# Attention, expert layers and a gated MLP on one core: one early load for the hash, smaller first pieces, gate and identity in one product

## The chip, the cores and the metric

One core of one Trainium2 chip runs the whole program in one launch. The time is the device time in microseconds, taken as the median over runs. The engines are TensorE (PE in the rows, its weight loads PEld), VectorE (DVE), ScalarE (ACT), GpSimd (POOL) and the queue engine SyncE (SP), which only issues transfers.

## What is computed

Three layers follow each other, all in float32:

```python
q_bits = (einsum('bhsd,dk->bhsk', q, proj) > 0)      # 6 hash bits, k alike
mask = q_bucket[:, :, :, None] == k_bucket[:, :, None, :]
scores = where(mask, scale * q @ k.T, -1e9)           # B=2, H=8, S=768, D=64
x = softmax(scores) @ v                               # 1536 tokens of 512
noisy = x @ w_gate + log1p(exp(x @ w_noise)) * noise  # 8 experts, best two
x = sum over the two: weight * relu(x @ w1[e]) @ w2[e]
h = x @ w_in;  out = (h * sigmoid(1.702 * h)) @ w_out
```

## The kernel before

**Attention** works on eight pairs of heads (`n` = 0 to 7, heads `j` = 0, 1 in a pair). Scores are products of float32r parts: `u1`, `v1` (scaled q and k) hold the high parts on 128 partitions, `u2`, `v2` the corrections on 64 partitions and, on 12 more, the hash bits, scaled so that a differing bit puts a score out of reach. One step `g` (96 in all) takes one block of 128 queries of one head against all 768 keys: `a_score` issues two products with `u1`, `v1` and two with `u2`, `v2` (L310), `a_soft` reduces the maximum on DVE (L322) and makes a scale and a bias (L323, L324), `a_exp` runs the exponential on ACT (L333), `a_trans` turns the result with six transposes on PE (L350) and copies them out on ACT or DVE (a string `COPIES` says which), `a_av` multiplies with v (L360), 12 products for a query block of both heads, each two instructions in the trace. Scores run two steps ahead of the transposes.

The order on every engine is written out by hand: `attention` holds a table of (step, function, arguments), and within a step the table's calls follow the fixed calls above. An engine runs its instructions in that order.

**The first pair** has functions of its own (`z_...`), since its loads have just started. `a_load(0)` issues k of head 0 and then the hash matrix `projq` on ACT's queue, and on SP's queue the first half of q of head 0, k of head 1 and the other three halves of q. A column of ones (`sgn`) comes by POOL's queue. `z_mm` is the hash product of one half of one q or k (L191, 64 rows by 32 columns of PE, 384 columns moved), `z_bits` makes the bits of it on DVE (L263), for q with a scaling on ACT behind (L266). `z_u1`, `z_lo`, `z_u2`, `z_v1`, `z_v2` make the parts. Ahead of all this PE multiplies a matrix of ones with itself 27 times (`WARM`, L533).

**The later pairs** use `a_hash`, `a_hb` (bits on DVE, half of them scaled on ACT, L207) and DMAs that move the bits into `u2`, `v2`.

**The output steps** `a_xt` run 18 times: 15 take three row blocks, three (at the end) one. For each block a product of the attended values `xu` (weights of PE) with 32 columns of gate weights (L398, two instructions each) and one transpose of `xu` by the identity (L401, one instruction) go to one bank; DVE scales both by the softmax sums.

**Routing** of a group of 384 tokens runs in DVE operations between steps; POOL scatters token rows to expert slots by indirect DMAs (`r_scatter`).

**Expert 0** starts inside attention's scope: `f_load` fetches its 384 rows with one DMA, `f_tr` transposes them by column block (12 transposes, L999) into two tiles, ACT makes the high part (L793), DVE the rest (L794), and `f_s1` multiplies (through `m_mm1`, L1020 to L1022). Experts 1 to 7 and the last MLP follow; they hold PE from 265 us to the end.

Of the kernel before, what the change touches and what calls it, by code (L numbers as in the profile page):

```python
# [34 lines left out]
WARM = 27  # L35
W0 = 28
# [5 lines left out]
class Kernel:  # L42
# [19 lines left out]
    def consts(self):  # L62
        nc, a = self.nc, self.a
        p = self.cpool
        self.sc = self.t(p, [128, 2], F32, "sc")
# [3 lines left out]
        self.sgn = self.t(p, [128, 1], F32, "sgn")  # L69
        nc.gpsimd.dma_start(self.sgn, a["sgn"])  # L70
        self.ident = self.t(p, [128, 128], F32, "ident")
        make_identity(nc, self.ident)

    def consts2(self):
        nc, a = self.nc, self.a
        p = self.cpool
        self.wg = self.t(p, [128, 4, 32], F32, "wg")
        nc.gpsimd.memset(self.wg, 0.0)
        for j in range(2):
            for x, nm in enumerate(("w_gate", "w_noise")):  # L80
                c0 = 16 * j + 8 * x
                nc.sync.dma_start(self.wg[64 * j:64 * j + 64, :, c0:c0 + 8],
                                  a[nm].rearrange("(c j p) e -> j p c e", j=2, p=64)[j])
        self.tri = self.t(p, [128, 128], BF, "tri")
        nc.vector.memset(self.tri, 1.0)
        nc.gpsimd.affine_select(self.tri, self.tri, pattern=[[1, 128]], compare_op=ALU.is_gt,
                                fill=0.0, base=0, channel_multiplier=-1)
        self.ones = self.t(p, [128, 128], BF, "ones")
        nc.vector.memset(self.ones, 1.0)
# [4 lines left out]
        nc.vector.tensor_copy(self.iotb, self.iota)  # L94
        nc.vector.memset(self.iotb[:, 0:1], float(E * NT))
        self.over = self.t(p, [128, 9], F32, "over")
        nc.vector.memset(self.over, 0.0)
        nc.vector.memset(self.over[:, 0:1], float(CAP - CAPB))
        nc.vector.memset(self.over[:, 8:9], float(CAP - CAPA))
        self.slot = self.t(p, [128, 12, 2], I32, "slot")  # L100
        self.ysl = self.t(p, [128, 12, 2], I32, "ysl")
        self.slot2 = self.t(p, [128, 12, 2], I32, "slot2")
        self.wgt = self.t(p, [128, 12, 2], F32, "wgt")
        self.nz = self.t(p, [128, 12, 8], F32, "nz")
        nc.sync.dma_start(self.nz, a["noise"].rearrange("(i p) e -> p i e", p=128))
        self.spacer = self.t(p, [1, 1], F32, "spacer")
        self.macc = self.t(p, [128, 9], BF, "macc")
        nc.vector.memset(self.macc, 0.0)
# [20 lines left out]
    def a_load(self, n):  # L129
# [58 lines left out]
    def hash_mm(self, ps, r, hf, t):  # L188

        rs = slice(64 * hf, 64 * hf + 64)  # L190
        return self.nc.tensor.matmul(ps[r:r + 32, :], self.projq[rs, :], t[rs, hf * HALF:(hf + 1) * HALF],  # L191
                                     start=True, stop=True)
# [10 lines left out]
    def a_hb(self, n, hf):  # L203
        nc = self.nc
        hb = self.hb[n][:, hf * HALF:(hf + 1) * HALF]
        nc.vector.tensor_scalar(hb, self.hps[hf], 0.0, self.sgn[:, 0:1], op0=ALU.is_gt, op1=ALU.add)
        nc.scalar.activation(hb[64:128, :], hb[64:128, :].bitcast(F32), AF.Copy, scale=BIG)  # L207
        self.use(dve=0.62, act=0.4)
# [19 lines left out]
    def z_u1(self, j, hf, e):  # L228
        cs = slice(hf * HALF, (hf + 1) * HALF)
        self.z_mul(e, self.uv[0, j][0][:, cs], self.raw[0]["q", j][:, cs], self.sc[:, 0:1])  # L230

    def z_lo(self, j, hf, e):
        cs = slice(hf * HALF, (hf + 1) * HALF)
# [3 lines left out]
    def z_u2(self, j, hf, e):  # L237
        cs = slice(hf * HALF, (hf + 1) * HALF)
        self.z_mul(e, self.uv[0, j][2][0:64, cs], self.raw[0]["q", j][0:64, cs], SCALE)

    def z_v1(self, j, e):
        self.z_mul(e, self.uv[0, j][1], self.raw[0]["k", j], self.sc[:, 1:2])

    def z_v2(self, j, e):
        u1, v1, u2, v2 = self.uv[0, j]
        self.z_sub(e, v2[0:64, :], self.raw[0]["k", j][0:64, :], v1[0:64, :].bitcast(F32))
# [12 lines left out]
    def z_bits(self, nm, j, hf):  # L259
        nc = self.nc  # L260
        r = 64 * (nm == "k") + 32 * j
        d = self.uv[0, j][2 if nm == "q" else 3][64:76, hf * HALF:(hf + 1) * HALF]
        o = nc.vector.tensor_scalar(d, self.zps[hf][r:r + 12, :], 0.0, self.sgn[r:r + 12, 0:1], op0=ALU.is_gt, op1=ALU.add)  # L263
        self.z_other(o, r, hf, False)
        if nm == "q":
            nc.scalar.activation(d, d.bitcast(F32), AF.Copy, scale=BIG)  # L266
# [5 lines left out]
    COPIES = "aaddaaadaaaddaaaaaaaaadaadadadadaaddaddadaaadaaaaaadadaaaaaaaaaadddaaddaaadaaddaaaadaaadaadddaadaaaadaaaddaadadaaddadadaaaaaaaaaadaadaddaaaaaaaddaadaaaaaaaddaaaaaaaddaaaddaaaaaaaaaaaadaaaaaaaaaaaadaaddaaaaadaaa"  # L272
# [28 lines left out]
    def a_score(self, g):  # L301
# [6 lines left out]
        for (l, r, kk, st) in ((u1, v1, 128, True), (u2, v2, K2, False)):  # L308
            for hf in range(2):
# [64 lines left out]
    def a_xt(self, u, c=None, spare=False):  # L374
# [20 lines left out]
        pt = ps[:, 0:nch * 128].rearrange("p (c d) -> p c d", c=nch)  # L395
        pl = ps[:, 384:384 + nch * 32].rearrange("p (c j e) -> p c j e", c=nch, j=2)
# [1174 lines left out]
```

## Time and profile before

| What | us |
|---|---|
| median of three runs (865.27 to 866.52) | 865.75 |
| the profiled execution, device time | 869.32 |
| its span, first to last instruction | 867.5 |
| PE busy | 848.0 |
| DVE busy | 524.3 |
| ACT busy | 443.6 |
| POOL busy | 220.0 |

The mean granted clock of PE is 0.988 of full speed. The profile cuts the span into stretches and tells for each how long an engine was busy, which clock PE was granted and what the DMA engines moved; the chain that ended last follows the last instruction back, at each step to the one that released it. Attention ends at about 262 us.

### The profile page before, as it was taken

To read this page: it belongs to the slowest core of one execution; us is meant where nothing else is said; L and a number is where in the kernel's file an instruction comes from. 1 tells how busy PE (TensorE), PEld (TensorE's weight loads), DVE (VectorE), ACT (ScalarE), POOL (GpSimd) and SP (SyncE) were. 2 spreads that over 40 slices of the span, in tenths; PEclk is the share of its full clock that TensorE was granted. 3 is DMA by queue.
4 is the path that set the end of the run, shared out by engine and by line. 5 is a ranking of instruction groups with operands and counts; after the bars stand their busy time and mean duration, and the time that the engine had idled before them with its cause. 6 is when DMAs were issued, how large, how long until landed. Compare 5 with 4: busy or idle time off the path is not lost.

```text
span 867.5 us, 15554 instructions
## 1 busy us (share of the span) xinstructions
PE 848.0 (98%) x6116; PEld 777.5 (90%) x6116; DVE 524.3 (60%) x1068; ACT 443.6 (51%) x787; POOL 220.0 (25%) x227
## 2 busy tenths in 40 slices
PE   8999999999989999999999999999999999999997
PEld 5888898788979999999999999978898988989896
DVE  5877778676765598989898897756512121212120
ACT  4977988788763444443544344447423231314130
POOL 4421654486024000000000000026524141503040
PEclk6999999999999999999999999999999999999999
DMA  5747654533135577887878687638301010100000
GB/s 187 223 162 247 168 157 138 181 105 111 37 111 209 195 261 240 290 253 234 296 237 279 223 268 233 213 119 321 98 25 49 25 49 25 42 33 1 25 1 28
DMA packets 52382, 132.29 MB, mean 152 GB/s; under 512 B 8912, under 2 KB 11024, under 8 KB 52304
## 3 DMA queue, kind: packets, MB, share of 16 engines
q1 hardware_dynamic: 43968, 109.64, 38.6%
q0 software_dynamic: 6992, 20.37, 7.7%
q10 hardware_dynamic: 1344, 1.23, 0.4%
q8 instruction: 50, 0.82, 0.4%
q14 instruction: 28, 0.23, 0.1%
HBM read 92.05 MB, written 35.39 MB: 147 GB/s over the span
## 4 chain that ended last, share of the span: by engine, by line
PE 95%; ACT 1%; DMA 1%; DVE 1%; issue 1%; POOL 0%; ACTq 0%; DVEq 0%; POOLq 0%
PE g L1292 15%; PE s L310 9%; PE av L360 8%; PE p L350 7%; PE y L1044 5%; PE y L1046 5%; PE y L1045 5%; PE h L1020 5%; PE h L1021 5%; PE h L1022 5%; PE o L1337 4%; PE o L1339 4%; PE o L1338 4%; PE t L1063 2%; PE t L999 1%; PE m L398 1%
## 5 line engine op out<-in xcount | busy, mean ns | idle before, releaser
L322 DVE TENSOR_REDUCE mx<-s 128x1 f32<-128x768 f32 x96 | 91.5, 954 | 30.0 <-PE s L310 28.2
L333 ACT ACTIVATE P<-s,sm 128x768 f32<-128x768 f32 x96 | 95.3, 992 | 26.4 <-DVE sm L324 23.6
L1301 POOL TENSOR_TENSOR gl<-sg,gh 128x512 fp32r<-128x512 f32 x48 | 66.2, 1380 | 162.1 <-ACT gh L1300 162.1
L1245 POOL DMA_INDIRECT yg<-ys,ysl x24 | 25.8, 1074 | 304.1 <-DVE wl L893 297.7
L310 PE MATMUL s<-v,u 76*128 76x384 f32 (+1 forms) x384 | 95.6, 371 | 1.3 <-DVE v L263 0.8
L1297 DVE TENSOR_TENSOR sg<-g,sg 128x512 f32<-128x512 f32 x48 | 33.2, 692 | 93.5 <-ACT sg L1296 89.2
L350 PE MATMUL p<-ident,P 128*128 128x128 f32 x576 | 81.7, 278 | 4.4 <-ACT hh L281 2.4
L310 PEld LDWEIGHTS s<-v,u 76*128 76x128 f32 (+1 forms) x384 | 64.6, 195 | 17.9 <-issue 11.9
L350 PEld LDWEIGHTS p<-ident,P 128*128 128x128 f32 x576 | 69.7, 143 | 10.9 <-ACT hh L281 3.3
L1027 ACT ACTIVATE hh<-h 128x416 fp32r<-128x416 f32 x56 | 29.0, 518 | 72.7 <-PE h L1022 72.3
L1044 PE MATMUL y<-hh,wh 128*128 128x416 f32 (+1 forms) x144 | 51.2, 355 | 0.0
L1296 ACT ACTIVATE sg<-g 128x512 f32<-128x512 f32 x48 | 28.7, 599 | 41.9 <-PE g L1292 39.6
L1046 PE MATMUL y<-hh,wl 128*128 128x416 f32 (+1 forms) x144 | 49.8, 346 | 0.0
L1045 PE MATMUL y<-hl,wh 128*128 128x416 f32 (+1 forms) x144 | 49.7, 345 | 0.0
L1300 ACT ACTIVATE gh<-sg 128x512 fp32r<-128x512 f32 x48 | 30.3, 631 | 31.0 <-DVE sg L1297 30.2
L1028 DVE SCALAR_TENSOR_TENSOR hl<-h,hh 128x416 fp32r<-128x416 f32 x56 | 32.9, 588 | 14.2 <-ACT hh L1027 14.1
L1292 PE MATMUL g<-bth,wh 128*128 128x256 f32 x144 | 40.2, 279 | 0.0
L1292 PE MATMUL g<-btl,wh 128*128 128x256 f32 x144 | 40.1, 279 | 0.0
L1292 PE MATMUL g<-bth,wl 128*128 128x256 f32 x144 | 40.1, 278 | 0.0
L1292 PE MATMUL g<-x2h,wh 128*128 128x256 f32 x144 | 39.7, 277 | 0.0
L1044 PE MATMUL y<-hh,wxh 128*128 128x416 f32 (+1 forms) x112 | 39.6, 354 | 0.0
L1292 PE MATMUL g<-x2h,wl 128*128 128x256 f32 x144 | 39.6, 276 | 0.0
(327 smaller groups left out, 2492.4 us busy)
## 6 DMA issues: line engine op xcount, KB each, us to landing
ws<-in_w SPq DMA_DIRECT2D x40, 512.0 KB, 5.4
d_in<-in_w SPq DMA_DIRECT2D x32, 512.0 KB, 5.0
bth<-in_w SPq DMA_DIRECT2D x16, 512.0 KB, 4.1
btl<-in_w SPq DMA_DIRECT2D x16, 512.0 KB, 4.7
wd<-d_o SPq DMA_DIRECT2D x32, 256.0 KB, 4.0
xs<-xeh SPq DMA_DIRECT2D x13, 512.0 KB, 5.7
rawk<-in_kT SPq DMA_DIRECT2D x15, 384.0 KB, 4.2
rawq<-in_qT SPq DMA_DIRECT2D x14, 384.0 KB, 4.9
```

Source lines behind the costliest of these rows:

```text
L310: nc.tensor.matmul(ps[:, hf, :HALF], l[:kk, q0:q0 + 128], r[:kk, hf * HALF:(hf + 1) * HALF], start=st, stop=not st)
L322: nc.vector.tensor_reduce(mx, ps[:, :, :HALF], axis=AX.XY, op=ALU.max, negate=True)
L333: nc.scalar.activation(P, ps[:, :, :HALF], AF.Exp, bias=sm[:, 1:2], scale=sm[:, 0:1], accum_out=self.RS[u][:, c, j, 0:1])
L350: nc.tensor.transpose(ps[:, kb, :], P[:, hf, kb * 128:(kb + 1) * 128], self.ident)
L360: nc.tensor.matmul(self.pa[64 * j:64 * j + 64, c * 128:(c + 1) * 128], self.vt[n][:, kb, 64 * j:64 * j + 64], PT[:, j, kb, :], start=(kb = ...
L1020: nc.tensor.matmul(ps, wh[:, fs], xh[:, d, :n], start=(d == 0), stop=False)
L1021: nc.tensor.matmul(ps, wh[:, fs], xl[:, d, :n], start=False, stop=False)
L1044: nc.tensor.matmul(ps, wh[:, ds_], hh[:, f, :], start=(f == 0), stop=False)
L1045: nc.tensor.matmul(ps, wh[:, ds_], hl[:, f, :], start=False, stop=False)
L1046: nc.tensor.matmul(ps, wl[:, ds_], hh[:, f, :], start=False, stop=(f == 7))
L1292: nc.tensor.matmul(ps[:, x, :], self.units[NU + 4 * (f // 8) + d][w][:, fs], y[:, d, :], start=(i == 0), stop=(i == 11))
L1301: nc.gpsimd.tensor_tensor(gl[:, fo, :], g, gh[:, fo, :].bitcast(F32), op=ALU.subtract)
```

## The change

**Loads.** One array `hdr` (66 columns: the hash matrix twice, a threshold and a factor for the bits) is the first DMA of ACT's queue, then k of both heads. SP's queue brings the four halves of q, then one array `cst` with gate weights, identity and noise, then the second pair's loads, then v. The five small loads of gate weights and noise and the identity built on POOL are gone. DVE negates six columns of `hdr`.

**Bits.** Threshold and factor are read from `hdr`, so one DVE operation makes scaled bits; the scalings on ACT (L266, L207) are gone.

**Order of the start.** `WARM` is 37 and the ones are DVE's first instruction. The first half of q is worked on in pieces of 128 and 256 columns (`PIECE`), k in two halves. `keep_on` puts 26 more products of the ones behind the hash product of q's second half. Further calls of the table move by a step or two, one subtraction of pair 1 goes from DVE to POOL, and `COPIES` has other letters.

**Output steps.** One product of 160 columns (32 of gate weights and the identity side by side) takes the place of L398 and L401.

**Expert 0.** Three DMAs fetch its rows, `f_tr` transposes and splits by row tile, and the first product group takes its eight products with the high part first. The store of the last group's rows moves behind `f_s1(0)`.

```diff
-WARM = 27
+WARM = 37
...
+        self.ones = self.t(p, [128, 128], BF, "ones")
+        nc.vector.memset(self.ones, 1.0)
...
-        nc.gpsimd.dma_start(self.sgn, a["sgn"])
-        make_identity(nc, self.ident)
+        nc.vector.tensor_scalar(self.hdr[:, NB:32 + NB], self.hdr[:, NB:32 + NB], -1.0, None, op0=ALU.mult)
...
+        cst = self.t(p, [128, 384 + 96], F32, "cst")
+        nc.sync.dma_start(cst, a["cst"])
+        self.iw = [cst[:, 192 * (c // 2) + 32 * (c % 2):192 * (c // 2) + 32 * (c % 2) + 160] for c in range(4)]
+        self.ident = cst[:, 32:160]
...
-            nc.scalar.dma_start(raw["k", 0], a["kT"][b, 2 * p])
-            nc.scalar.dma_start(self.projq, a["projq"])
-            for nm, j, c0, c1 in (("q", 0, 0, HALF), ("k", 1, 0, S), ("q", 1, 0, HALF), ("q", 0, HALF, S), ("q", 1, HALF, S)):
+            nc.scalar.dma_start(self.hdr, a["hdr"])
+            for j in range(2):
+                nc.scalar.dma_start(raw["k", j], a["kT"][b, 2 * p + j])
+            for nm, j, c0, c1 in (("q", 0, 0, HALF), ("q", 1, 0, HALF), ("q", 0, HALF, S), ("q", 1, HALF, S)):
...
+    PIECE = (slice(0, 128), slice(128, HALF), slice(HALF, S))
...
+    def keep_on(self, n):
+        ps = self.t(self.ps_p, [128, 128], F32, "p")
+        for _ in range(n):
+            self.nc.tensor.matmul(ps, self.ones, self.ones, start=True, stop=True)
...
+        o = nc.vector.tensor_scalar(d, ps, self.hdr[r:r + 12, 64:65], self.hdr[r:r + 12, 65:66], op0=ALU.is_gt, op1=ALU.mult)
...
-            nc.scalar.activation(d, d.bitcast(F32), AF.Copy, scale=BIG)
...
         for x in range(nch):
-            nc.tensor.matmul(ps[:, 384 + 32 * x:416 + 32 * x], xu[:, x * 128:(x + 1) * 128], self.wg[:, p, :],
-                             start=True, stop=True)
-        for x in range(nch):
-            nc.tensor.transpose(pt[:, x, :], xu[:, x * 128:(x + 1) * 128], self.ident)
+            nc.tensor.matmul(pc[:, x, :], xu[:, x * 128:(x + 1) * 128], self.iw[p], start=True, stop=True)
...
+        for i in range(3):
+            self.nc.sync.dma_start(t[:, i, :], x[i * 128:(i + 1) * 128, :])
...
+        for i, (o, w) in enumerate(self.tiles(0)):
...
+            for d in range(4):
+                nc.tensor.transpose(pt[:, d, :], self.xrow[0][:, i, d * 128:(d + 1) * 128], self.ident)
+            nc.scalar.activation(xh[:, :, o:o + w], pt[:, :, :w], AF.Copy)
...
+        if e == f == 0:
+            mm.sort(key=lambda m: m[2] is xl)
```

The table's effect on the order, at the three places that count. **PE, from the first hash product to the third block of scores.** `m` and `av` are the two banks of hash results, `s` a block of scores, `p` a spare bank. Before:

```order
L191 MATMUL m_194<-rawq_1_105,projq_80 32x384
L191 MATMUL av_96<-rawk_1_106,projq_80 32x384
L191 MATMUL m_194<-rawk_1_106,projq_80 32x384
L191 MATMUL m_194<-rawk_1_108,projq_80 32x384
L191 MATMUL av_96<-rawk_1_108,projq_80 32x384
L310 MATMUL s_212<-v_1_190,u_1_185 128x384 x2
L310 MATMUL s_212<-v_1_191,u_1_186 128x384 x2
L191 MATMUL m_194<-rawq_1_107,projq_80 32x384
L310 MATMUL s_230<-v_1_190,u_1_185 128x384 x2
L310 MATMUL s_230<-v_1_191,u_1_186 128x384 x2
L191 MATMUL av_96<-rawq_1_105,projq_80 32x384
L310 MATMUL s_249<-v_1_192,u_1_187 128x384 x2
```

Now:

```order
L185 MATMUL m_189<-rawk_1_106,hdr_80 32x384
L185 MATMUL m_189<-rawq_1_105,hdr_80 32x384
L185 MATMUL av_96<-rawk_1_106,hdr_80 32x384
L185 MATMUL m_189<-rawk_1_108,hdr_80 32x384
L185 MATMUL av_96<-rawk_1_108,hdr_80 32x384
L185 MATMUL m_189<-rawq_1_107,hdr_80 32x384
L320 MATMUL s_216<-v_1_185,u_1_180 128x384 x2
L320 MATMUL s_216<-v_1_186,u_1_181 128x384 x2
L320 MATMUL s_233<-v_1_185,u_1_180 128x384 x2
L320 MATMUL s_233<-v_1_186,u_1_181 128x384 x2
L185 MATMUL av_96<-rawq_1_105,hdr_80 32x384
L253 LDWEIGHTS ones_116
```

A sixth hash product (q of head 1, first half) now stands ahead of the first scores, two blocks of scores stand together, and 26 products of the ones stand between them and the third.

**SP, its first transfers.** `rawq`, `rawk` with 1_105 to 1_108 are the first pair's, with 2_ the second's. Before:

```order
L138 DMA rawq_1_105<-in_qT 128x384
L138 DMA rawk_1_108<-in_kT 128x768
L138 DMA rawq_1_107<-in_qT 128x384
L138 DMA rawq_1_105<-in_qT 128x384
L138 DMA rawq_1_107<-in_qT 128x384
L82 DMA wg_127<-in_w_gate 64x4x8
```

Now:

```order
L131 DMA rawq_1_105<-in_qT 128x384
L131 DMA rawq_1_107<-in_qT 128x384
L131 DMA rawq_1_105<-in_qT 128x384
L131 DMA rawq_1_107<-in_qT 128x384
L77 DMA cst_124<-in_cst 128x480
L137 DMA rawq_2_302<-in_qT 128x768
```

k of head 1 has gone to ACT's queue (third there), and the second pair's loads stand where the small gate loads stood.

**PE, from the last output steps to expert 0.** Before:

```order
L398 MATMUL m_3782<-wg_127,xu_3746 128x32
L401 MATMUL m_3782<-ident_122,xu_3746 128x128
L398 MATMUL p_3792<-wg_127,xu_3780 128x32
L401 MATMUL p_3792<-ident_122,xu_3780 128x128
L999 MATMUL s_3804<-ident_122,xrow_1_3653 128x128 x6
L999 MATMUL s_3813<-ident_122,xrow_1_3653 128x128 x6
L1020 MATMUL s_3836<-xeh_3802,wh_1403 128x320
L1021 MATMUL s_3836<-xel_3803,wh_1403 128x320
```

Now:

```order
L410 MATMUL m_3753<-cst_124,xu_3718 128x160
L410 MATMUL p_3761<-cst_124,xu_3751 128x160
L818 MATMUL s_3771<-cst_124,xrow_1_3624 128x128 x4
L818 MATMUL s_3778<-cst_124,xrow_1_3624 128x128 x4
L818 MATMUL p_3785<-cst_124,xrow_1_3624 128x128 x4
L1048 MATMUL s_3806<-xeh_3769,wh_1412 128x320
L1048 MATMUL s_3806<-xeh_3769,wl_1413 128x320
```

One product has taken the place of two, the transposes come in three groups of four, and the products with the low part `xel` have moved behind eight with the high part.

## Rows read from the trace of the kernel before

**Rows 1.** The page, part 1: engine, busy us (share of the span), instructions.
```profile
PE 848.0 (98%) x6116; PEld 777.5 (90%) x6116; DVE 524.3 (60%) x1068; ACT 443.6 (51%) x787; POOL 220.0 (25%) x227
```

**Rows 2.** Timeline of PE at the start: start, length, line, shapes, [idle before <-releaser].
```profile
1.65 2.99 PE L533 MATMUL s<-ones 128*128 128x128 bf16 x27 [1.65 <-DVE ones L89]
6.34 0.48 PE L191 MATMUL m<-rawq,projq 64*32 64x384 f32 x1 [1.70 <-DMA projq<-in_projq]
...
7.13 0.62 PE L310 MATMUL s<-v,u 128*128 128x384 f32 x2
8.58 1.13 PE L310 MATMUL s<-v,u 76*128 76x384 f32 x2 [0.83 <-DVE v L263]
```

**Rows 3.** Windows of the start: length, busy PE, PEld, DVE, ACT, POOL, PEclk, DMA, GB/s.
```profile
2.00:4.00 2.00, 2.00 (x22) 2.00 (x20) 0.34 (x6) 1.05 (x1) 1.18 (x6) 1.00 0.96 260
4.00:6.00 2.00, 0.64 (x7) 0.44 (x5) 0.88 (x2) 1.18 (x2) 0.00 (x0) 1.00 0.89 328
6.00:8.00 2.00, 1.41 (x12) 0.49 (x12) 0.81 (x3) 0.44 (x2) 1.66 (x1) 0.96 0.83 215
7.80:8.00 0.20, 0.00 (x0) 0.00 (x0) 0.18 (x1) 0.18 (x1) 0.20 (x1) 0.61 0.61 34
...
21.40:21.60 0.20, 0.20 (x2) 0.20 (x1) 0.20 (x1) 0.20 (x1) 0.00 (x0) 0.76 0.00 0
```

**Rows 4.** Chain that ended last, 9 to 26 us: start, length, work.
```profile
9.71 1.42 PE m L191 x2
11.13 1.58 PE s L310 x4
...
15.70 1.28 PE p L350 x6
...
22.81 0.70 PE s L310 x4
23.51 0.66 PE p L350 x6
24.17 1.46 PE av L360 x24
```

**Rows 5.** DVE's groups by form, 0 to 60 us: busy us, mean ns, idle before.
```profile
L322 DVE TENSOR_REDUCE mx<-s 128x1 f32<-128x768 f32 x20 | 19.1, 953 | 5.8 <-PE s L310 5.4
L324 DVE TENSOR_SCALAR sm<-mx 128x1 f32<-128x1 f32 x19 | 3.9, 204 | 0.0
...
L263 DVE TENSOR_SCALAR v<-m,sgn 12x384 fp32r<-12x384 f32 x2 | 1.2, 620 | 0.1
```

**Rows 6.** POOL's groups by form, 0 to 60 us: busy us, mean ns, idle before.
```profile
L226 POOL TENSOR_TENSOR v<-rawk,v 64x768 fp32r<-64x768 f32 x3 | 5.4, 1813 | 4.3 <-ACT v L221 3.1 <-ACT v L179 1.1
```

**Rows 7.** Chain that ended last, one output step of three row blocks.
```profile
35.41 0.59 PE m L398 x6
36.00 0.36 PE m L401 x3
```

**Rows 8.** Chain that ended last, from the end of attention to expert 0's first products.
```profile
262.53 0.67 PE s L999 x6
...
263.22 0.71 ACT xeh L793
...
263.96 0.84 DVE xel L794
...
264.84 0.41 PE s L1020
```

**Rows 9.** Chain that ended last, a stall in the middle of attention.
```profile
158.95 2.06 PE s L310 x4
...
161.58 1.54 PE p L350 x6
163.12 2.33 PE av L360 x24
```

More of the change, by code (lines that the diff above doesn't have):

```diff
@@ L8 @@
 from concourse._compat import with_exitstack
-from concourse.masks import make_identity
 F32 = mybir.dt.float32
@@ L76, in consts2 @@
         p = self.cpool
[L77 to L83, printed above, removed]
+        cst = self.t(p, [128, 384 + 96], F32, "cst")
+        nc.sync.dma_start(cst, a["cst"])
+        self.iw = [cst[:, 192 * (c // 2) + 32 * (c % 2):192 * (c // 2) + 32 * (c % 2) + 160] for c in range(4)]
+        self.ident = cst[:, 32:160]
+        self.nz = cst[:, 384:480].rearrange("p (i e) -> p i e", i=12)
         self.tri = self.t(p, [128, 128], BF, "tri")
[L85 to L86 removed]
+        nc.gpsimd.affine_select(self.tri, self.ones, pattern=[[1, 128]], compare_op=ALU.is_gt,
                                 fill=0.0, base=0, channel_multiplier=-1)
[L88 to L89 removed]
         self.iota = self.t(p, [128, 8], F32, "iota")
@@ L308, in a_score @@
         for (l, r, kk, st) in ((u1, v1, 128, True), (u2, v2, K2, False)):
+            if g == 0 and not st:
+                self.warm(W1)
             for hf in range(2):
@@ L412, in a_xt @@
         self.use(dve=1.0)
-        if p == 3:
+        if p == 3 and bq < 3:
             self.x_store(bq, c0, nch)
@@ L530, in attention @@
         LA = 2
-        ps = self.t(self.ps_s, [128, 2, 512], F32, "s")
-        for i in range(WARM):
-            nc.tensor.matmul(ps[:, 0, :128], self.ones, self.ones, start=True, stop=True)
+        self.wps = self.t(self.ps_s, [128, 2, 512], F32, "s")
+        self.warm(WARM)
         self.a_uv(0)
@@ L571, in attention @@
-            (2, self.z_u1, 1, 1, "a"),
-            (2, self.z_u2, 1, 1, "v"),
+            (-1, self.keep_on, 26),
+            (-1, self.z_bits, "q", 0, 2),
+            (-1, self.z_u2, 1, 1, "a"),
+            (0, self.z_lo, 1, 1, "p"),
+            (0, self.z_u2, 0, 2, "v"),
+            (0, self.a_load, 1),
+            (0, self.z_lo, 0, 2, "p"),
+            (1, self.z_mm, "q", 1, 1),
+            (1, self.z_bits, "q", 1, 2),
+            (2, self.z_u1, 1, 2, "a"),
+            (2, self.z_u2, 1, 2, "v"),
@@ L770, in attention @@
         self.f_s1(0)
+        self.x_store(3, 0, 3)
         self.r_do(3, "noisy", "top", "index", "pick")
         self.f_s1(1)
+        self.f_s1(2)
         self.r_do(3, "rank", "place", "slots")
@@ L776, in attention @@
         self.r_do(3, "weights")
-        for f in range(2, 8):
+        for f in range(3, 8):
             self.f_s1(f)
@@ L781, in f_load @@
         t = self.t(self.ap, [128, 3, DM], F32, "xrow0", 1)
-        self.m_rows(0, t, self.nc.sync)
+        x = self.rows(self.xs, 0)
+        for i in range(3):
+            self.nc.sync.dma_start(t[:, i, :], x[i * 128:(i + 1) * 128, :])
         self.xrow[0] = t
@@ L1017, in m_mm1 @@
         fs = slice(f * 128, (f + 1) * 128)
-        for d in range(4):
-            wh, wl = self.units[8 * e + d]
-            nc.tensor.matmul(ps, wh[:, fs], xh[:, d, :n], start=(d == 0), stop=False)
-            nc.tensor.matmul(ps, wh[:, fs], xl[:, d, :n], start=False, stop=False)
-            nc.tensor.matmul(ps, wl[:, fs], xh[:, d, :n], start=False, stop=(d == 3))
+        mm = [(d, w, y) for d in range(4) for w, y in ((0, xh), (0, xl), (1, xh))]
+        if e == f == 0:
+            mm.sort(key=lambda m: m[2] is xl)
+        for i, (d, w, y) in enumerate(mm):
+            nc.tensor.matmul(ps, self.units[8 * e + d][w][:, fs], y[:, d, :n], start=(i == 0), stop=(i == 11))
     def m_h(self, e, f, ps):
@@ L1504, in run @@
             with ExitStack() as c2:
-                self.projq = self.t(self.cpool, [128, 32], F32, "projq")
+                self.hdr = self.t(self.cpool, [128, 66], F32, "hdr")
                 self.attn_pools(c2)
@@ L1535, in layout @@
     w64.append(w)
-    sgn = np.zeros((128, 1), np.float32)
+    hdr = np.zeros((128, 66), np.float32)
+    for x in (0, NB, 32, 32 + NB):
+        hdr[:, x:x + NB] = np.concatenate([inp["proj"]] * 2)
     for g in range(4):
-        for r in range(2 * NB):
-            first = r < NB
-            sgn[32 * g + r, 0] = -1.0 if first == (g >= 2) else 0.0
-    projq = np.zeros((2, 64, 32), np.float32)
-    projq[:, :, :2 * NB] = np.concatenate([inp["proj"]] * 2, axis=1)
+        r = 32 * g + NB * (g < 2)
+        hdr[r:r + NB, 64] = -np.finfo(np.float32).tiny
+    hdr[:64, 65], hdr[64:, 65] = BIG, -1.0
+    wg = np.zeros((2, 64, 4, 2, 2, E), np.float32)
+    for j in range(2):
+        for x, nm in enumerate(("moe_w_gate", "moe_w_noise")):
+            wg[j, :, :, j, x] = inp[nm].reshape(4, 2, 64, E)[:, j].transpose(1, 0, 2)
+    nz = inp["moe_noise"].reshape(12, 128, E).transpose(1, 0, 2).reshape(128, 12 * E)
+    wg = wg.reshape(128, 4, 32)
+    eye = np.eye(128, dtype=np.float32)
+    cst = np.concatenate([wg[:, 0], eye, wg[:, 1], wg[:, 2], eye, wg[:, 3], nz], axis=1)
     return {
```

206 lines of the change are left out of this document (105 added, 101 removed).

## The prediction

> **What bounds the kernel now.** First the page: PE is busy for 848.0 us of a span of 867.5, 98%, DVE for 60% and ACT for 51% [rows 1]. So only what shortens PE's own work, or its few idle stretches, can shorten the kernel. Then the windows, for the rate of that work: the granted clock falls between 7.8 and 8.0 us (0.61 in that window) and comes back between 21.4 and 21.6 (0.76) [rows 3]; in between the windows show 0.50, so for 13.6 us PE is on the lower of its two levels, 1.2 instead of 2.4 GHz. Then the timeline of PE, for what it did before the fall: 27 products of the ones to 4.64 us, an idle wait of 1.70 us for the hash matrix, 0.8 us of hash products, 0.6 us of scores, another wait of 0.83 us for DVE's bits [rows 2]. Last the chain of waits: from 8.6 us it lies on PE almost without a gap, and the same steps cost twice as much under the lower level: four score instructions 1.58 us against 0.70, six transposes 1.28 against 0.66 [rows 4]. The first attended block ends at 24.17 + 1.46 = 25.63 us. That is the mark against which I measure the start.
>
> **The start: loads.** The wait for the hash matrix goes, since `hdr` is first in its queue. What is late next is k of head 1: its two hash products stand ahead of the first scores, and it is now third in ACT's queue instead of second in SP's. Before, all first hash products were done when the scores began at 7.13 [rows 2]. The pair's loads are 4 x 192 + 2 x 384 KB, 1.57 MB; the windows from 2 to 6 us moved 0.52 + 0.66 = 1.18 MB [rows 3], so if k of head 1 is the very last to arrive, the other 0.39 MB at 328 GB/s put it at 7.2 us. Ends: 6.3 (it comes as early as before) and 9.0 (half that rate and some delay). I take 7.2.
>
> **The start: order.** Three hash products side by side take some 0.5 us (each 0.48, rows 2): 7.7. The first two score instructions take 0.62 us: 8.3. The next two need the bits and v2. Of bits, DVE has about three operations of 0.62 us or less behind hash products that no longer wait [rows 5]; of v2, POOL has half operations of 1.81 / 2 = 0.9 us, both done by about 7.8 [rows 6]. So these two scores run at 8.3 to 9.4 at the lower level (1.13 us, rows 2); before they ended at 9.71. The clock will have fallen as before, for PE still waits before 7.2. Then, all at the lower level: the second block of scores 1.58 (11.0), a hash product 1.42 (12.4) [rows 4], and `keep_on`: 26 products of the ones at 2.99 / 27 = 0.111 us [rows 2], 2.9 us: 15.3. POOL's work for head 1 (four half operations and three smaller ones) ends before that.
>
> What does `keep_on` buy? In the trace of before, 27 such products were followed by hash products at the upper level (0.48 us for an instruction, where a pair takes 1.42 later), while 13 us of float32 work, three hash products on a part of the array among it, were not followed by a rise for long [rows 2 to 4]. So I expect the upper level from about 15.3 on. From there PE has, up to the mark: four blocks of scores at 0.70, four sets of transposes at 0.66, half of 1.42 for a hash product, and 1.46 of attended values: 2.80 + 2.64 + 0.71 + 1.46 = 7.61 [rows 4]. That ends at 22.9 instead of 25.63: **2.7 us won**. DVE must not be later than that: from 9.4 on it has six reductions of 0.95 with two small operations each, the longer 0.20, and three of 0.62, some 10 us with the copies at most a few more [rows 5], so it ends at about 21.
>
> **Output steps.** Before, three row blocks cost 0.59 + 0.36 = 0.95 us on the chain [rows 7]. Now each is one float32 product of 160 columns. Its price is not in the trace; the nearest row of its kind is the hash product, float32 and two instructions: 1.42 us for 384 columns at the lower level [rows 4], 0.71 at the upper, 1.85 ns a column, so 0.296 for 160 and 0.89 for three. The row of attended values gives the dear end: 12 products of 128 columns in 1.46 us, taken as pairs side by side, 0.243 a pair, 0.91 for three blocks. The transposes give the cheap end: 0.66 / 6 = 0.11 for an instruction of 128 columns, 0.1375 for 160, two for each product, 0.825 for three. I take 0.89, as the same kind: 0.06 for each three blocks, and there are 48 blocks, 16 times three: **1.0 us won**, between 0.6 and 2.0. The Trainium skill, "TensorE: Matmul & The Clock Gate", section "Terms", speaks against this edit: transposes have a mode of their own which is "4× faster for FP32", and a plain product with the identity does without it. By that, 128 columns would cost 4 x 0.12 us; the rows show 0.12 a transpose (0.94 ns a column) against 1.85 ns for a plain product, two to one. I keep the row; what the rule would make of the time is a rival below.
>
> **Expert 0.** PE ends its 12 transposes with 0.67 for the first six, and then stands until ACT (0.71) and DVE (0.84) have made both parts of the first half: products begin at 264.84 [rows 8]. By tile, four transposes take 0.45, so ACT starts at 262.98 and needs, at 0.71 for 640 columns, 0.57 + 0.57 + 0.29 and a few hundredths between: 264.55. The first eight products read high parts alone, so DVE's are not waited for. **0.2 us won.** Rows that come in three DMAs win nothing: no wait for them stands in the chain.
>
> **At nothing:** the ACT scalings that go (ACT is 51% busy and rarely ends a wait of PE), the subtraction on POOL (25% busy), the shifted calls, the store behind `f_s1(0)`, the second pair's loads ahead of v (v is used 13 us later). If the covers fail, they come out as one more stall of PE, which a rival prices.
>
> **Sum:** 2.7 + 1.0 + 0.2 = 3.9 us. The profiled execution took 869.32 us, a span of 867.5 and 1.8 around it; it stands 3.6 us above the median of the runs shown, 865.75. Against it the sum gives 865.4, against the median **861.8 us**. No change that can be measured means within 0.2%, 1.7 us.
>
> **Rivals.**
> - *The clock stays low.* If `keep_on` lifts nothing, its 2.9 us are spent for nothing and the level rises at 21.5 as before. From 15.3: 1.58 + 1.28 + 1.58 + 1.28 to 21.0, a hash product to about 22.1, then 0.70 x 2 + 0.66 x 2 + 1.46 to 26.3: 0.7 lost, in all 865.2, no change. For it speaks that the ones follow a hash product; against it that the ones at the start were followed by the upper level. If k of head 1 also comes at 9.0, 866 or a little more.
> - *The clock never falls.* With 37 products of the ones to about 5.2 and hash products right behind, PE's idle stretch is shorter than the 1.70 us of before. Then the second scores end near 9.0, and with 0.70, 0.71 and half of 2.9 and 7.61 the mark is at 19.5; DVE's 10 us and copies hold it at about 20.5: 5.1 won, in all 859.4. Against it: PE still waits for k of head 1.
> - *A stall more or less.* At 158.95 four score instructions took 2.06 us instead of 0.70, and the lower level that followed cost 1.54 instead of 0.66 and 2.33 instead of 1.46 [rows 9]: 3.1 us in all. No wait that the profile names explains it. A shifted order may lose it (858.7) or meet one more (864.9).
> - *The joined product is dear*, the other side. It decides at 0.317 us for a block (0.95 / 3). If a plain float32 product costs four transposes a column, 160 columns take 4 x 0.12 x 160 / 128 = 0.60, three blocks 1.80, and 16 such 13.6 us more: 876.4 with the other terms. This is the rule of the Trainium skill named above. Against it stands the hash product's row, half that dear.
>
> **Chances:** the forecast 0.56, the clock that never falls 0.12, a stall lost 0.06: faster 0.74. Low clock 0.08, one stall more 0.06, late k 0.04: no change 0.18. The dear product 0.05 and what I don't see 0.03: slower 0.08. The range goes from the never-falling clock with the cheap product (859.4 - 1.0, and something of a lost stall), 858.0, to the late k, 866.0; the forecast's own bounds are 860 to 863.5.
>
> **What would show it.** PEclk at 0.5 from about 8 to 15 us and at 1.0 behind, the first attended block ending near 22.9; output steps at 0.89 for three blocks in the chain; expert 0's first product 0.3 after ACT's second tile. If the level rises only past 20 us, or the output step shows over 0.95, the forecast is wrong; a third stall such as that of rows 9 would hide it.

## The result: 850.1 us, and the profile after

The kernel before took 865.5 us in this comparison (864.4 to 866.5, four runs), the changed one **850.1 us** (849.2 to 851.7, four runs): a ratio of 0.982, 95% interval 0.981 to 0.984. Forecast were 861.8 us and a range of 858 to 866. The sign was right; the gain is 15 us where 4 were expected. The profiled execution after took 851.66 us, a span of 850.0; its page:

```profile
PE 837.5 (99%) x6104; PEld 775.9 (91%) x6104; DVE 525.7 (62%) x1069; ACT 433.7 (51%) x771; POOL 222.6 (26%) x235
```

PE is busy for 10.5 us less than in [rows 1] and stands idle for 7 us less. The start, on PE's timeline after (columns as in rows 2):

```profile
1.15 4.13 PE L247 MATMUL s<-ones 128*128 128x128 bf16 x37 [1.15 <-DVE sc L68]
5.25 0.81 PE L185 MATMUL m<-rawk,hdr 64*32 64x384 f32 x1
...
7.80 0.51 PE L185 MATMUL m<-rawk,hdr 64*32 64x384 f32 x1 [1.23 <-DMA rawk<-in_kT]
...
8.57 1.67 PE L320 MATMUL s<-v,u 128*128 128x384 f32 x8
...
10.93 1.62 PE L253 MATMUL p<-ones 128*128 128x128 bf16 x26
...
19.88 1.53 PE L370 MATMUL av<-hh,v 128*64 128x128 f32 x24
```

k of head 1 landed at 7.76 us, later than the 7.2 forecast, but the clock did not fall: eight score instructions take 1.67 us where four took 1.58 in [rows 4], and the 26 ones 1.62 us, not 2.9. Ahead of that, by the durations, PE was still on the lower level: a product of the ones took 0.112 us there (4.13 / 37) against 0.062 later (1.62 / 26), a hash product 0.81 against 0.51. It was on the upper level by 7.8 us and stayed there through the start. The first attended block ends at 21.41 instead of 25.63 us: 4.2 us won. An output step and expert 0, on the chain that ended last after:

```profile
233.45 0.82 PE m L410 x6
...
246.47 0.70 DVE xel L820
...
247.31 4.77 PE s L1048 x31
```

Three row blocks cost 0.82 us against 0.95 in [rows 7]. Expert 0's first product starts only behind DVE's first subtraction, as in [rows 8], although its operands are there; the order of the products moved no wait. Its bank is the one that this subtraction was still reading, so the bank is the likely reason; that was not tried. One more edit belongs to expert 0: its third product group now stands ahead of the last routing.

**Where the time went by stage.** The marks are DVE's maximum of steps 10, 50 and 95 (L322, after L332), the end of the last output product, and expert 0's first product with `hh`, all from the timelines. The second column is the second profile of the kernel before, the third and fourth are experiments told below.

| Stage, us | before, first | before, second | start alone (e15) | old middle (e12) | after |
|---|---|---|---|---|---|
| to step 10 | 37.2 | 38.3 | 36.0 | 37.2 | 33.0 |
| steps 10 to 50 | 97.0 | 97.0 | 97.3 | 96.8 | 95.4 |
| steps 50 to 95 | 121.2 | 113.5 | 113.2 | 112.3 | 109.6 |
| to the last output product | 7.2 | 7.1 | 7.1 | 7.1 | 6.8 |
| to expert 0's second layer | 16.8 | 19.7 | 16.8 | 16.6 | 17.0 |
| to the end | 588.2 | 587.5 | 586.0 | 585.8 | 588.2 |
| span | 867.5 | 863.1 | 856.4 | 855.7 | 850.0 |

The first profile of before lost some 8 us between steps 50 and 95 that its second did not lose; rows 9 are a piece of that. The profile after has an accident of its own in the last stage. There PE waits 3.7 us in all for DVE's sums of gathered rows, and then the granted clock falls (a window, columns as in rows 3):

```profile
573.00:576.20 3.20, 3.20 (x14) 2.88 (x13) 2.25 (x3) 2.86 (x4) 2.28 (x3) 0.50 1.01 406
```

At the upper level the same work would take half of the 3.2 us, so this costs some 1.6 us (an estimate from the two to one of rows 4); in e12 and e15 the clock doesn't fall there. Single profiles differ by such accidents, so the parts below are told by medians and the places by the stages.

### The profile page after: what moved, and what is told of

It reads as the page before. It is cut to its first block, busy times and chain, and to the rows that moved or that the text cites. A ratio compares the mean times of both kernels' runs of the same rounds, so it can differ in the third digit from the quotient of the medians.

```text
span 850.0 us, 15512 instructions
## 1 busy us (share of the span) xinstructions
PE 837.5 (99%) x6104; PEld 775.9 (91%) x6104; DVE 525.7 (62%) x1069; ACT 433.7 (51%) x771; POOL 222.6 (26%) x235
## 4 chain that ended last, share of the span: by engine, by line
PE 96%; DMA 1%; DVE 1%; issue 0%; ACT 0%; POOL 0%; ACTq 0%; DVEq 0%; POOLq 0%
PE g L1318 16%; PE h L1048 15%; PE s L320 9%; PE av L370 8%; PE p L360 7%; PE y L1070 6%; PE y L1072 6%; PE y L1071 5%; PE o L1364 4%; PE o L1363 4%; PE o L1365 4%; PE s L1048 2%; PE t L1089 2%; PE m L410 2%; PE t L1025 1%; PE o L1343 1%
## 5 line engine op out<-in xcount | busy, mean ns | idle before, releaser
L332 DVE TENSOR_REDUCE mx<-s 128x1 f32<-128x768 f32 x96 | 91.6, 954 | 21.8 <-PE s L320 20.6
L1271 POOL DMA_INDIRECT yg<-ys,cst x24 | 25.4, 1059 | 302.1 <-DVE wl L919 295.7
L320 PE MATMUL s<-v,u 76*128 76x384 f32 (+1 forms) x384 | 92.5, 362 | 0.3
L360 PE MATMUL p<-cst,P 128*128 128x128 f32 x576 | 78.9, 273 | 0.0
L360 PEld LDWEIGHTS p<-cst,P 128*128 128x128 f32 x576 | 68.8, 141 | 4.1 <-ACT hl L289 0.2
L1318 PE MATMUL g<-x2l,wh 128*128 128x256 f32 x144 | 39.7, 280 | 0.0
```

What stands on the lines that cost most here:

```text
L320: nc.tensor.matmul(ps[:, hf, :HALF], l[:kk, q0:q0 + 128], r[:kk, hf * HALF:(hf + 1) * HALF], start=st, stop=not st)
L332: nc.vector.tensor_reduce(mx, ps[:, :, :HALF], axis=AX.XY, op=ALU.max, negate=True)
L360: nc.tensor.transpose(ps[:, kb, :], P[:, hf, kb * 128:(kb + 1) * 128], self.ident)
L1318: nc.tensor.matmul(ps[:, x, :], self.units[NU + 4 * (f // 8) + d][w][:, fs], y[:, d, :], start=(i == 0), stop=(i == 11))
```

## Experiments

Each time stands beside runs of the kernel before on the same chip. On three chips those took 865.0 to 865.3 us, on the fourth, where the last two kernels ran, 873.6.

### The middle: order, letters, ACT operations

**e1** puts the old table back from step 33 on.

> The changed kernel with the table of the kernel before from step 33 on (all calls behind the ninth zero fill); start, joined product, COPIES and expert 0 stay as changed. Step by step, the changed kernel is 4.2 us ahead when the start is done, some 1.3 us more comes evenly with the output steps, and 11 to 12 us come in four places in the middle of attention (steps 56 to 59, 60 to 66, 72 to 73, 93 to 94) where the kernel before had stalls. Theory A, the order of the table from step 33 on made these stalls: they come back, 861 to 862 us. Theory B, they came of something else (the letters of COPIES, the ACT scalings, the joined product, the shift by the start): 850 to 851 us. Between: some stalls belong to the order and some don't.

851.4 us (850.4 to 852.9). **e2** gives the new table to the kernel before.

> The kernel before with the changed table from step 33 on, and nothing else of the change. Theory A (the order from step 33 on made the stalls): they go, 853 to 855 us. Theory B (something else): 865 us as before. If e1 shows stalls and this one too, it takes two parts of the change together to lose them.

865.5 us, ratio 1.001 [0.999, 1.002]. The order alone made no stall and removes none: theory A falls.

**e4**: the old `COPIES` string.

> The changed kernel with the letters of COPIES of the kernel before, 44 of some 210 places different, which say whether ACT or DVE copies a block of transposed probabilities. Theory D, a stall in the middle is DVE or ACT late with copies at a place where routing loads DVE: some of the 11 to 12 us come back, 853 us or more, in the steps 56 to 94. Otherwise 850 to 851 us.

852.9 us, a spread of 0.4: the letters are worth 2.8 us, 1.9 of it in steps 50 to 95 (111.5 against 109.6). That the time shows in these steps fits theory D, DVE or ACT late with copies; no wait was traced to a letter.

**e5** puts an ACT operation behind the bits of the later pairs:

```diff
         nc.vector.tensor_scalar(hb, self.hps[hf], self.hdr[:, 64:65], self.hdr[:, 65:66], op0=ALU.is_gt, op1=ALU.mult)
+        nc.scalar.activation(hb[64:128, :], hb[64:128, :].bitcast(F32), AF.Copy, scale=1.0)
```

> The changed kernel with the ACT operation on the hash bits of pairs 1 to 7 put back (14 operations of 64 x 384, here with a factor of 1). It costs ACT 0.52 us each, 7.3 us in all, and it stands in ACT's order behind bits that DVE makes late: in the kernel before with the new table, ACT idled 2.9 us in front of ten of them, and copies of transposed probabilities, for which PE waits, stood behind. Theory E, these operations held back the copies and exponentials in the middle and so stalled PE: 853 to 857 us. Theory F, ACT has room, the stalls came of the early start or of accidents of an execution: 850 to 851 us.

854.8 us (853.0 to 856.3): 4.7 more. 1.0 of the profile's 4.6 us came at the start, 1.1 in steps 10 to 50, 2.3 in steps 50 to 95. The 1.0 is not the operation's, which first runs at 28.9 us, when the 1.0 us are already lost: in this execution k of head 0 came later and PE was on the lower level for longer. PE's timeline of e5, where eight score instructions take 2.28 us instead of 1.67:

```profile
8.24 0.84 PE L185 MATMUL m<-rawk,hdr 64*32 64x384 f32 x1
...
9.02 2.28 PE L321 MATMUL s<-v,u 128*128 128x384 f32 x8
```

So by the profile the operation costs 3.6 us. The chain that ended last shows how, in e5:

```profile
162.65 0.53 ACT hb L201
...
163.20 1.07 ACT P L344 x2
...
164.69 0.52 ACT hb L201
...
165.23 0.35 ACT u L169
...
166.07 0.48 ACT hh L290
...
166.60 0.93 PE p L361 x6
```

And the same steps after, some 3 us earlier:

```profile
162.41 0.81 PE s L320 x4
163.23 0.66 PE p L360 x6
163.89 1.46 PE av L370 x24
```

Without the operation the chain lies on PE alone. With it, it runs over ACT: ACT works in order, waits there for bits that DVE makes late (3.8 us in all, in front of 6 of the 14), and exponentials and copies stand behind. Theory E holds in the changed kernel.

**e6** takes the operations out of the kernel before (bits by threshold and factor, a DVE operation more at the start).

> The kernel before with bits by threshold and factor (one DVE operation), so that the ACT operations on bits of pairs 1 to 7 are gone; the first pair keeps one, its loads, order and output steps stay. DVE has one small operation more at the start. Theory E: PE's stalls in the middle shrink, 858 to 861 us. Theory F: 864 to 866 us.

868.0 us: slower, ratio 1.003 [1.001, 1.004], as neither theory said. Steps 50 to 95 did shrink (111.7 against 113.5 us), but the new operation waited for the hash load (PE stood 2.3 us ahead of the first products), PE waited 2.0 us for expert 0's rows, and the stage to the end took 592.1 us. **e10** leaves the start alone and adds the new table:

> The kernel before without the ACT operations on the bits of pairs 1 to 7 and with the changed table from step 33 on; start, output steps, COPIES and expert 0 as before. In e6 the middle was won (3.5 us against e2) and lost again, by a dearer start (2.1 us, an operation that waited for the hash load) and because expert 0's rows then landed after PE was ready for them (2.0 us of waiting, and a lower clock behind). The start is left alone here. Theory E (the ACT operations cost 3.4 us): 861 to 862 us if the rows are there in time; 863 to 865 us if the wait for the rows takes it back, to be seen as a wait of PE for xrow. Theory F: 865 us, with no such wait.

865.3 us, ratio 1.000 [0.999, 1.001], without a wait for the rows: up to expert 0's second layer it is 5.0 us ahead of before's second profile, but 2.9 of these are a wait of that profile and what follows it (told at expert 0), and 1.0 is the start, where the code is the same. Then the stage to the end takes 591.3 us instead of 587.5. **e11**, with the new letters too:

> As e10, with the changed letters of COPIES: all of the change between the start and expert 0 but the joined product. e4 priced the letters at 2.8 us, e5 the ACT operations at 4.7 of which 1.0 came at the start. If these add up: 858.5 to 859.5 us. If the letters only fit the changed kernel's order, no better than e10. If the wait for expert 0's rows decides, 862 to 865 us.

862.6 us, ratio 0.996 [0.994, 0.998], and again 590.1 us in the last stage (one of its ten runs took 1186.2 us, which is not explained). Part of what these three lose there, 1.6 us, is explained below (the place of the weight tiles). In e10 most of the rest is the clock, which fell behind a wait of 2.9 us for gathered rows, where e9's did not; a window of e10:

```profile
578.00:582.00 4.00, 3.36 (x12) 2.84 (x13) 2.03 (x3) 1.32 (x2) 3.39 (x6) 0.57 0.93 320
```

Why it falls in some executions and not in others stays open. With the 1.6 us taken out, e10 would stand some 2 us below e2, which lacks only the removal of the ACT operations (theory E holds there too, at less than half the price), and e11 4.3 us below the kernel before. **e12** is the whole old middle in the changed kernel:

> The changed kernel with the ACT operations on bits, the table from step 33 on and the COPIES of the kernel before: start, joined product and expert 0 remain of the change. By the sum of e1, e4 and e5 (1.3, 2.8 and 3.7 to 4.7 us): 858 to 859 us. If the three hide one another (they all load ACT at the same places), 855 to 857 us; if they make each other worse, 860 us or more. The gain of start, output steps and expert 0 by the profile is 4.2 + 1.3 to 2.1 + about 1 us, so 857.5 to 858.5 us are expected from that side.

854.6 us (854.1 to 857.5). The middle is worth **4.5 us**, less than its parts by themselves (1.3, 2.8, 4.7): they hide one another. The 4.3 of e11, where the same parts are given to the kernel before, agrees.

### Output steps

**e3**: 

```diff
-            nc.tensor.matmul(pc[:, x, :], xu[:, x * 128:(x + 1) * 128], self.iw[p], start=True, stop=True)
+            nc.tensor.matmul(pc[:, x, 128 * odd:128 * odd + 32], xu[:, x * 128:(x + 1) * 128],
+                             self.iw[p][:, 128 * odd:128 * odd + 32], start=True, stop=True)
...
+            nc.tensor.transpose(pt[:, x, :], xu[:, x * 128:(x + 1) * 128], self.ident)
```

> The changed kernel with the joined product taken apart again: a product with 32 columns and a transpose for each block, as before. Its own price by the traces is 0.95 against 0.82 us for three blocks, 16 times: 2.1 us, so 852.2 us if it is only that. If the joined product also keeps the stalls away (theory C: its copies and banks come earlier), 858 us or more. If the transposes beside other work cost nothing, 850 us.

851.2 us (850.6 to 852.3): the joined product is worth 1.1 us, 1.5 by the stages (0.6 and 0.9 in the two long ones). The term of 1.0 stands.

### The start

**e7**: `WARM` 42 in the kernel before.

> The kernel before with 42 products of the ones at the start instead of 27, so that PE's idle wait of 1.70 us for the hash matrix is filled and nothing else changes. Theory G, the lower clock of the start follows this idle wait: the granted clock stays at 1.0, the first attended block ends some 3 to 4 us earlier and the time is 861 to 862 us. Theory H, it follows the float32 work or the second wait of 0.83 us: the clock falls all the same and the time is 865 us or a little more.

860.7 us, ratio 0.995 [0.994, 0.997]. The time is what theory G gave, the mechanism only half: the wait for the hash matrix is gone, the clock still fell, but later, and step 10 came 1.4 to 2.6 us earlier than in the profiles of before, of 4.4 us won by the medians. **e8** removes `keep_on`.

> The changed kernel without the 26 products of the ones of keep_on. In the trace after they stand while PE would wait for DVE's work anyway. If they only fill that wait and the clock stays at 1.0 without them: 850 us, no change. If they keep the clock up: it falls near 12 us and comes back some ten us later, 853 to 856 us. If they hold PE up: 848 to 849 us.

851.2 us. In its profile PE waits for POOL; one row of PE's waits (total, times, longest):

```profile
PE s L320 <- POOL u L219: 1.8, 1, 1.8
```

And the granted clock is lower; a window of e8, columns as in rows 3:

```profile
12.00:16.00 4.00, 2.88 (x12) 2.82 (x13) 3.80 (x9) 3.70 (x8) 2.46 (x4) 0.70 0.05 17
```

After, this window reads 1.00. The ones fill a wait and hold the clock, for 1.2 us by the medians and 1.3 at step 10. **e15** leaves of the change only the start (the loads, the table to step 32 and the constants they need):

> The changed kernel with the middle (ACT operations on bits, table, COPIES), the output steps and expert 0 as before: what remains of the change is the start (loads, bits of the first pair, order and pieces, products of the ones) and constants that come by one load. By the trace's 4.2 us: 861 us. If the clock falls in an execution as it did in the profile of e12, that execution gains nothing at the start. If the start also moves accidents of the middle, as filling the idle wait did in e7 (1.3 us at the start, 4.3 by the medians): 857 to 860 us. By subtraction (865.1 less 15, plus 4.5, 1.1 and expert 0's 2 to 3): 858 us.

857.5 us (855.1 to 858.9), ratio 0.991 [0.989, 0.992]: **7.7 us**, in an execution whose profile even shows a fallen clock:

```profile
8.00:12.00 4.00, 3.84 (x16) 2.07 (x16) 3.65 (x8) 1.41 (x3) 3.02 (x4) 0.72 1.03 408
12.00:16.00 4.00, 4.00 (x29) 3.48 (x29) 2.49 (x6) 2.68 (x6) 3.06 (x5) 0.50 0.11 41
```

e12's profile shows one too; its timeline at the second group of hash products:

```profile
7.98 0.84 PE L185 MATMUL m<-rawk,hdr 64*32 64x384 f32 x1 [1.72 <-DMA rawk<-in_kT]
```

There the start wins nothing over before's first profile (37.2 us to step 10). e1 is the third of the ten profiles with this start whose clock fell (0.50 from 7.4 to 10.6 us). Waits for the same load of 1.23 us (after) and 1.6 us (e13) were not followed by a fall, waits of 1.24 us (e1) and 1.6 us (e15) were: the length alone doesn't tell. **e16** puts eight ones into that wait:

> The changed kernel with eight more products of the ones between the hash products of head 0 and those of head 1, where PE waits 1.2 us for k of head 1 (0.5 to 0.9 us of work, so most of the wait is filled). In the profile of e12 this wait was 1.72 us and the clock fell, in the changed kernel 1.23 us and it didn't. If executions of the changed kernel with a fallen clock are rare: 850 us, no change. If they are common: 848 to 849.5 us and less spread. If the eight products delay the hash products of head 1: up to 0.5 us more.

849.7 us (849.1 to 852.2), the same as the changed kernel. No version tried beats it measurably.

### Expert 0

**e9** is the kernel before, profiled a second time.

> The kernel before, unchanged, for a second profile of it. The first one (span 867.5 us) lost 3.1 us at step 94, 3.0 at steps 72 and 73 and 3.1 at the stall of rows 9 against the profile with the new table, whose time is the same by the medians. If these are accidents of one execution, some are missing here and the span is 862 to 865 us; if they belong to the kernel, they show again and the span is about 867 us.

864.9 us, a span of 863.1: the stalls of the first profile are accidents. Now PE came to expert 0's rows earlier and had to wait; a row of PE's waits in e9:

```profile
PE s L999 <- DMA xrow<-xs: 2.0, 1, 2.0
```

And the chain that ended last, behind that wait:

```profile
257.91 0.89 PE s L999 x6
```

Behind the wait six transposes take 0.89 us instead of 0.67 [rows 8], and the second layer begins 19.7 instead of 16.8 us after the last output product. **e14** gives the new code for expert 0 to the kernel before, **e13** the old code to the changed kernel.

> The kernel before with the changed code for expert 0 alone (three DMAs, transposes and splits by row tile, products with the low part last, the store behind the first product group, a third product group ahead of the last routing). By the prediction's term: 0.2 us less, 864.9 us, which can't be told from no change. Theory R (in most executions of the kernel before PE waits some 2 us for the rows): 861.5 to 863.5 us, and no wait for xrow in the profile.

> The changed kernel with the code of the kernel before for expert 0: one DMA for its rows, transposes by column block, products in the old order, the last rows stored ahead of the first product group. By the prediction's term (only the two splits stood in the way): 0.2 us more, 850.3 us. Theory R (PE would now come to the rows before they have landed, since attention behind the last scatter is shorter): PE waits for xrow, 852 to 854 us, with a lower clock behind the wait if it is long.

e14: 862.6 us, ratio 0.997 [0.995, 0.998], no wait for `xrow` in its profile: 2.6 us won. e13: 850.6 us, 0.5 more and no wait either. In e9 the one DMA takes 5.1 us to land, in e14 the three take 3.2 (median); in the changed kernel the last scatter starts 1.3 us earlier against step 95 than in e9, and even the single DMA is in time. Theory R fits from the side of before, not from the other: two edits seem to cover the same wait.

How often the kernel before has this wait isn't known. Of ten profiles with the old code for expert 0, e9 and e6 show 2.0 us, e11 0.7, and seven 0.2 or none, among them e2, which is no faster by the medians. So the 2.6 us aren't shown to be this wait alone; e14's third product group, which stands earlier, was not tried by itself. The same wait is missing in e7 and e15, with the old code (17.0 and 16.8 us to the second layer, 19.7 in e9): part of what these two won may be that, and not the start's.

### The place of the weight tiles

The last MLP isn't touched by the change. Yet from the product with nine columns (after its first output group) to PE's last instruction it took 223.3 to 223.4 us in the kernel before, e2, e7 and e14, 221.9 in the changed kernel, e1, e3, e4, e8, e12, e13, e15 and e16 (222.3 in e5), and 225.0 in e6, e10 and e11. In the built programs the first weight tile begins at byte 19,200 of a partition (before), 19,584 (after), and at 19,360 or 19,616 in those three: constants of another size lie ahead. The change also has 32 unused bytes there (`pad_c`, not in the diff shown). **e17** adds 384 unused bytes to the kernel before, **e18** takes the 32 away from the changed one; no instruction differs. All tiles behind the constants move together.

> The kernel before with 384 unused bytes behind its constants, so that weight tiles begin where they begin in the changed kernel; no instruction differs. Theory P (the place of the tiles in the memory sets how fast the last MLP's products run): the last MLP's stretch goes from 223.4 to 221.9 us and the stretch ahead of it from 26.1 to 25.7, 863.4 us in all against 865.1. Theory Q (something else of the program, such as where its instructions stand): 223.4 us there, 865 us in all.

> The changed kernel without the 32 unused bytes among its constants, so that the weight tiles begin 32 bytes earlier (as an odd multiple of 32, as in the three variants with 225.0 us); no instruction differs. Theory P: the last MLP's stretch goes from 221.9 to some 225 us, 853 us in all or a little more. Theory Q: 221.9 us there, 850 us in all.

e17: 222.0 us in that stretch, 871.2 us in all, ratio 0.998 [0.996, 1.000], which alone is hardly clear of noise. e18: 225.5 us there. The first and the last product of the stretch on PE's timeline, in before:

```profile
638.78 0.18 PE L1397 MATMUL u<-macc,ones 128*128 128x9 bf16 x1
...
861.83 0.28 PE L1317 MATMUL o<-w3h,gl 128*128 128x256 f32 x1
```

in e17:

```profile
640.90 0.18 PE L1398 MATMUL u<-macc,ones 128*128 128x9 bf16 x1
...
862.59 0.28 PE L1318 MATMUL o<-w3h,gl 128*128 128x256 f32 x1
```

after:

```profile
623.23 0.18 PE L1423 MATMUL u<-macc,ones 128*128 128x9 bf16 x1
...
844.85 0.28 PE L1343 MATMUL o<-w3h,gl 128*128 128x256 f32 x1
```

and in e18:

```profile
640.46 0.18 PE L1422 MATMUL u<-macc,ones 128*128 128x9 bf16 x1
...
865.71 0.28 PE L1342 MATMUL o<-w3h,gl 128*128 128x256 f32 x1
```

One group of PE by form (busy us, mean ns, idle before) from 620 to 845 us, in before:

```profile
L1337 PE MATMUL o<-wxh,gh 128*128 128x512 f32 x70 | 28.5, 407 | 0.0
```

in e17:

```profile
L1338 PE MATMUL o<-wxh,gh 128*128 128x512 f32 x73 | 29.4, 402 | 0.0
```

after:

```profile
L1363 PE MATMUL o<-wxh,gh 128*128 128x512 f32 x64 | 25.7, 401 | 0.0
```

and in e18:

```profile
L1362 PE MATMUL o<-wxh,gh 128*128 128x512 f32 x72 | 29.3, 406 | 0.0
```

Moved by unused bytes alone, the stretch goes from 223.3 to 222.0 us and from 221.9 to 225.5: theory P is shown. The mean of one group (407 or 401 ns) goes along, but it doesn't order the versions as the stretch does (406 in e18), and which of the moved tiles matters isn't shown. With the stretch ahead of it, from the first output group (26.1 against 25.7), the place is worth 1.8 us. It is in e15's 7.7; its opposite, 1.6, is in what e6, e10 and e11 lost.

On that chip e18 took 872.5 us, as much as the kernel before there (873.6). Most of its loss isn't the place: steps 50 to 95 took 125.2 us, with waits that name no releaser, on its chain:

```profile
187.06 2.36 issue
...
190.66 1.49 issue
```

e17 lost 8.1 us against before's second profile in the same steps. What stops the engines there, why e18 met more of it, and how the changed kernel itself does on that chip, stays open.

## Why the prediction was wrong

**The sum**, by the medians of kernels that contain each other: 865.2 before, 857.5 with the start alone (7.7 us, 1.8 of it the place of the tiles), 854.6 with the joined product and expert 0 as well (2.9: 1.1 for the product by e3, some 1.8 left for expert 0), 850.1 with the middle (4.5). The 1.8 for expert 0 and the start's 5.9 are remainders of medians, and the line between them isn't sharp (see the end of Expert 0). Beside the forecast's 2.7, 1.0, 0.2 and nothing, the start is short by 3.2 us, the product by 0.1, expert 0 by 1.6, the middle by 4.5, and the place by 1.8.

- *The step that failed most: "At nothing".* The ACT operations were costed by ACT's share (51%) and because ACT "rarely ends a wait of PE". The share in [rows 1] is one of the whole span; in steps 50 to 95 the bits, the weight splits and the copies queue in ACT's order, and one operation that waits holds all behind it (e5). Together with the order and the letters of `COPIES`, for which the prediction has no term, this is 4.5 us (e12). I had named the cover and not looked at the stage in which it is thinnest.
- *The start: mechanism wrong, 2.7 us where the trace shows 4.2.* I let the clock fall and `keep_on` lift it. It did not fall; the rival that it never falls (0.12) was right for this execution, and its mark of 20.5 was near the measured 21.4, with DVE's operations setting it as that rival said. In e12 and e15 the forecast's own path came about: the clock fell, the 26 ones took 2.95 and 2.96 us (2.9 forecast), the upper level was back at 17.9 and 16.6 us (15.3 forecast, 21.5 before), and the first attended block ended at 25.2 and 24.0 us (22.9 forecast). That the ones lifted it isn't shown: in e7, without `keep_on`, the level is back at 17.2. By medians the start gives about 5.9 without the place. Against before's second profile step 10 comes 5.3 us earlier (33.0 against 38.3); what is left may be the wait at expert 0.
- *Output steps: right*, 1.0 against 1.1 (e3) and the cheap end, 0.82 for three blocks. The Trainium skill ("TensorE: Matmul & The Clock Gate", "Terms") calls the transposes' own mode four times faster for float32; the estimate by that rule was 1.80 us for three blocks. The measured 0.82 decides against it.
- *Expert 0: 0.2 was the wrong wait.* "Rows that come in three DMAs win nothing: no wait for them stands in the chain" held for one execution that had lost time ahead of it. In the second profile the wait is 2.0 us, and 2.6 are won by all of the new code (e14), on the way to the changed kernel some 1.8. The part that was priced, the split by row tile, won nothing (2.5 us from the last output product to the first product, 2.3 before): "DVE's are not waited for" failed, PE waited for DVE's first subtraction all the same.
- *The stall of rows 9* was given as lost or met, 3 us either way. It is an accident of one execution and no part of the median's gain.
- *What was in no term*: the constants' size. 1.8 us came from where the weights lie.

## What to carry to other kernels

An operation of a half idle engine is not free when it waits: read in each stage what stands behind it in its engine's order. A load with no wait in a profile has a margin; read that margin, since whatever shortens the work ahead spends it. And when constants or buffers change size, compare a stretch that the change doesn't touch: if its products run at another rate, tiles may have moved. Unused bytes that move them back tell, and the difference has to be taken out before the rest is explained.

## What the runs showed of the hardware

- The same products ran up to 1.6% slower by where their tiles begin (221.9 to 225.5 us for a stretch of the last MLP), without any wait to be seen. The three slow places (225.0 to 225.5 us: 19,360, 19,616 and 19,552 bytes) are odd multiples of 32, the two others (19,200 and 19,584) are not; no further place was tried.
- A granted clock of 1.00 at the start of a profile need not be the upper level. PE's timeline of e9:

```profile
10.37 1.49 PE L191 MATMUL m<-rawq,projq 64*32 64x384 f32 x2
11.79 1.65 PE L310 MATMUL s<-v,u 128*128 128x384 f32 x4
```

And a window of it, columns as in rows 3:

```profile
12.00:16.00 4.00, 4.00 (x10) 2.33 (x11) 2.91 (x8) 2.74 (x6) 0.43 (x1) 1.00 0.94 375
```

These are the durations of 1.2 GHz under a granted clock of 1.00. The same instructions in the first profile of before, where the clock reads 0.50:

```profile
9.64 1.49 PE L191 MATMUL m<-rawq,projq 64*32 64x384 f32 x2
11.06 1.65 PE L310 MATMUL s<-v,u 128*128 128x384 f32 x4
```

The trace of e9 holds no clock record ahead of 23.2 us, that of the profile after none ahead of 6.3 us, and the windows read 1.00 where there is no record. The Trainium skill ("TensorE: Matmul & The Clock Gate", "Seeing it yourself") warns that clock events in a trace can be unreliable. What these runs show is narrower: at the start they can be missing. The duration of a known product tells the level.
